# A new order of all steps in a fused attention and MLP kernel

## The chip, the cores and the metric

The kernel runs on one core of a Trainium2 chip. Its time is the device time of one execution in microseconds; three executions of the kernel before took 575.28, 575.72 and 575.73 us, median 575.72. The profiled execution has a span of 574.3 us from the first recorded instruction to the last; no other time of that execution is given, so the 1.4 us between span and median are what lies around the span.

## The reference

The input is q, k, v (batch 4, 8 heads, 768 positions, 64 dimensions) and two weights. Each query attends to the keys within 15 positions of it, and to 24 summaries, one for each block of 32 positions: the elementwise maximum of the block's keys, and the mean of its values. The attention's output, 3072 tokens by 512, goes through a GELU MLP with 2048 hidden columns.

```python
k_sum = k.reshape(B, H, nb, block, D).max(axis=3)
v_sum = v.reshape(B, H, nb, block, D).mean(axis=3)
scores_l = scale * np.matmul(q, k.transpose(0, 1, 3, 2))
mask_l = np.abs(pos[:, None] - pos[None, :]) < window
scores_s = scale * np.einsum('bhsd,bhnd->bhsn', q, k_sum) + np.log(block)
scores_all = np.concatenate([np.where(mask_l, scores_l, -1e9), scores_s], axis=-1)
a = np.exp(scores_all - scores_all.max(axis=-1, keepdims=True))
a = a / (a.sum(axis=-1, keepdims=True) + 1e-09)
x = np.matmul(a, np.concatenate([v, v_sum], axis=2))   # then to (B*S, H*D)
h = x @ w_in
out = (0.5 * h * (1.0 + erf(h / sqrt(2)))) @ w_out
```

## The kernel before

The order of all work is written by hand. ORDER is a string of 1675 step names; the program walks it once, and each step issues its few instructions. Every engine then runs its own instructions in that order: TensorE (PE), VectorE (DVE), ScalarE (ACT), GpSimd (POOL), and SyncE (SP), which issues the DMAs. An engine waits when an operand is not ready, or when the buffer that it writes is still in use; the work behind it on that engine then waits too. Buffers are few: one PSUM tile each for scores (pss), for values (psv), for sums (psd) and for the MLP's second product (pso), three for its first (psh), and four SBUF tiles of 4 KB a partition (f4k) that hold scores, maxima and raw weights in turn.

*Attention* is cut into 24 units u, each of one batch, four heads and 256 queries. Units 0 to 5 (batch 0) are computed in float32: f_mask and f_scores (TensorE, lines 656 and 688), evac (ACT copies the scores to SBUF, line 772), maximum (GpSimd, partition_all_reduce, line 785), then either m_shift (TensorE subtracts the maximum in PSUM, line 736) and m_exponent, or shift (VectorE, line 790) and exponent (ACT, line 793), f_sums and f_values (TensorE, lines 710 and 702). Later units split each operand into a float16 high and low part and multiply three times (scores, values, sums: lines 756, 838, 854; the low parts q_lo, k_lo, p_lo, v_lo on VectorE). The norm_ steps divide by the sums: norm_take and norm_spread transpose on VectorE, norm_cross copies on ACT, norm_rec and norm_mult (line 888) are VectorE's. norm_mult reads psv and so frees it. x_hi (ACT) and x_lo (VectorE, line 895) split the result for the MLP. load_vs copies the value means beside the values; for batch 0 it is a GpSimd copy (line 625), or an ACT copy in s_load_vs.

*The MLP* works on chunks c of 256 tokens, two units each. phase1 c i multiplies by 256 hidden columns (lines 915 to 917), gelu and g_hi run on ACT, g_lo on VectorE (line 933); phase2 c i multiplies by w_out (lines 1034 to 1036), store and put bring the result out. For the chunk pairs 2 to 5 the first product is done with seven instead of eight block products (sp, snap, comb, s_gelu, sg_hi, sg_lo), for the last pair the second product too (so, o_snap, o_sum, o_out, o_put).

*Weights* arrive as float64 and are cut to float32 bits on VectorE in three parts, wi_bits i 0 to 2 and wo_bits f 0 to 2: part 0 reads the raw words alone (line 386, one input), parts 1 and 2 read the raw words and the result so far (lines 391 and 395, two inputs). wi_hi and wo_hi (ACT), wi_lo and wo_lo (VectorE, lines 424 and 484) split them. This, the key summaries (prep_k, prep_k_end with a cast in line 527) and the attention of batch 0 lie in the first 105 us.

*fill* steps are three matmuls of ones each (line 337, 14 steps, and 16 such matmuls in the setup). Their result is not used.

Of the kernel before, what the change touches and what calls it, by code (L numbers as in the profile page):

```python
# [102 lines left out]
norm_mult 4, wo_bits 2 0, exponent 5, f_sums 5, prep_k_end 1 0, f_values 5, gelu 1 6, wo_bits 2 1, load_q 7, norm_take
5, wo_bits 2 2, k_lo 6, g_hi 1 7, g_lo 1 7, wo_hi 3, k_sums 1 0, wo_bits 5 0, wo_lo 3, phase1 0 6, g_lo 0 2, gelu 0 6,
g_hi 0 6, wo_bits 5 1, wo_hi 2, wo_lo 2, fetch_w_out 4 4, f_mask 6, wo_bits 4 0, wo_bits 4 1, norm_cross 5, norm_rec
5, phase1 1 2, gelu 0 7, wo_bits 4 2, wo_hi 4, wo_bits 5 2, wo_hi 5, prep_k_end 1 1, wo_lo 4, wo_lo 5, g_lo 1 4,
scores 6, fetch_v 1 0, phase2 0 1, phase2 0 3, norm_spread 5, load_k 7, s_k_hi 7, phase2 0 2, fetch_v 1 1, phase2 0 5,
g_hi 0 7, fetch_w_out 6 4, x_hi 4, fetch_w_out 7 5, x_lo 4, norm_mult 5, s_q_hi 7, prep_v 1 1, evac 6, maximum 6,
phase2 0 4, load_mask, x_hi 5, x_lo 5, load_v 7, f_mask 7, q_lo 7, gelu 1 2, k_sums 1 1, shift 6, exponent 6, phase1 2
3, g_lo 0 6, wo_bits 6 0, phase1 2 1, load_q 9, k_lo 7, gelu 2 3, wo_bits 7 0, wo_bits 6 1, scores 7, g_hi 1 2, g_lo 1  # L110
2, wo_bits 6 2, wo_bits 7 1, gelu 2 1, s_q_hi 9, wo_hi 6, g_lo 0 7, wo_lo 6, phase1 2 0, load_k 9, wo_bits 7 2, q_lo
9, phase1 2 4, s_k_hi 9, k_lo 9, fetch_v 1 3, gelu 2 0, g_hi 2 0, s_p_hi 6, wo_hi 7, wo_lo 7, phase1 2 6, load_q 11,
load_k 8, phase2 0 6, fetch_k 2 2, prep_v 1 0, g_hi 1 6, g_lo 2 0, s_q_hi 11, prep_v 1 3, q_lo 11, p_lo 6, phase2 0 7,
store 0 0, phase2 1 0, fetch_v 2 1, load_vs 6, load_q 8, evac 7, maximum 7, load_vs 7, s_k_hi 8, gelu 2 6, put 0 0,
g_lo 1 6, prep_v 2 1, sums 6, k_lo 8, fetch_k 2 0, gelu 2 4, g_hi 2 4, v_hi 6, scores 9, norm_take 6, phase2 1 2,
phase2 1 4, prep_k 2 2, shift 7, v_hi 7, v_lo 6, values 6, store 0 1, fetch_k 2 3, g_lo 2 4, g_hi 2 1, prep_k 2 0,
phase1 2 5, s_q_hi 8, q_lo 8, add_mask 9, v_lo 7, scores 8, exponent 7, s_p_hi 7, norm_cross 6, phase2 1 6, p_lo 7,
# [5 lines left out]
s_k_hi 10, phase2 1 5, x_lo 7, v_hi 9, maximum 11, phase1 3 0, v_lo 9, gelu 2 7, wt_add 1 0, wt_add 1 1, wt_add 1 2,
wt_hi 1, k_lo 10, sums 8, shift 11, values 8, s_p_hi 9, q_lo 10, norm_take 8, norm_cross 8, load_v 10, gelu 3 0, g_hi
3 0, wt_lo 1, fetch_k 3 1, load_q 12, load_vs 10, norm_rec 8, phase1 3 4, phase2 1 7, wt_add 5 0, p_lo 9, phase1 3 1,
norm_spread 8, norm_mult 8, put 1 0, g_lo 3 0, gelu 2 2, exponent 11, scores 10, wt_add 5 1, fetch_k 3 2, g_hi 2 2,
g_lo 2 2, prep_k 3 1, x_hi 8, store 1 1, wt_add 5 2, g_hi 2 7, g_lo 2 7, gelu 3 4, prep_k 3 2, values 9, wt_hi 5, sums
# [1216 lines left out]
```

## Time and profile before

| | us |
|---|---|
| median of three runs | 575.72 |
| lowest, highest | 575.28, 575.73 |
| span of the profiled execution | 574.3 |
| TensorE's last matmul ends (tail: ACT's copy, then the output's DMA) | 571.04 |

The share of the span in which an engine is busy says which one bounds the kernel; the waits of that engine say what holds it; the table by stretches says how near another engine comes to it in one part of the run. In a timeline each line gives the start, the duration, the engine, the line of the program, the operation, the tiles written and read, and the count of instructions that the line groups.

### The profile page before, as it was taken

How to read it: one execution, taken by the hardware profiler on the slowest of the kernel's cores; microseconds unless marked ns; L12 is line 12 of the kernel's file. 1: busy time of each engine (PE TensorE's matmuls, PEld its weight loads, DVE VectorE, ACT ScalarE, POOL GpSimd, SP SyncE). 2: the span in 40 equal slices, each digit the busy share in tenths (PEclk: the TensorE clock that was granted, in tenths of full speed). 3: DMA queues.
4: the chain of work that ended last, by engine and by line, in shares of the span. 5: the costliest groups of instructions: out<-in, count | busy, mean ns of one | idle time of the engine just before them, and what ended most of it. 6: DMA issues, size and time to landing. Idle time of an engine off the chain costs nothing.

```text
span 574.3 us, 13533 instructions
## 1 busy us (share of the span) xinstructions
PE 569.0 (99%) x5826; PEld 389.8 (68%) x5826; DVE 458.4 (80%) x617; ACT 379.8 (66%) x642; POOL 88.7 (15%) x42
## 2 busy tenths in 40 slices
...
GB/s 322 395 238 250 342 175 196 274 116 198 159 115 99 141 79 71 115 121 76 103 93 66 72 105 56 60 98 78 23 63 1 21 19 18 1 20 1 2 1 91
DMA packets 28652, 64.27 MB, mean 112 GB/s; under 512 B 2736, under 2 KB 7600, under 8 KB 28592
## 3 DMA queue, kind: packets, MB, share of 16 engines
...
q8 instruction: 45, 0.74, 0.5%
...
## 4 chain that ended last, share of the span: by engine, by line
PE 95%; DVE 4%; issue 1%; ACT 0%; POOL 0%; DVEq 0%; ACTq 0%; POOLq 0%
PE psy L986 15%; PE pso L1034 12%; PE pso L1035 12%; PE pso L1036 12%; PE psz L986 7%; PE psh L915 4%; PE psh L917 4%; PE psh L916 4%; PE psx L986 4%; PE pso_y L1199 4%; PE psv L838 3%; PE pss L756 3%; PE pss_x L1199 2%; PE pso_fill L337 2%; PE pss L688 1%; PE pso_fill_s L337 1%
## 5 line engine op out<-in xcount | busy, mean ns | idle before, releaser
L785 POOL PARTITION_ALL_REDUCE m<-s x23 | 77.4, 3370 | 303.5 <-DVE s L776 80.9
L1034 PE MATMUL pso<-w_out_h,gg 128*128 128x512 f16 x320 | 121.5, 380 | 0.0
L1035 PE MATMUL pso<-w_out_l,gg 128*128 128x512 f16 x320 | 121.3, 379 | 0.0
L1036 PE MATMUL pso<-w_out_h,gg 128*128 128x512 f16 x320 | 121.3, 379 | 0.0
L986 PEld LDWEIGHTS <-wt 128*128 128x128 f16 x768 | 74.4, 98 | 13.6 <-issue 1.1
L916 PE MATMUL psh<-xos,ww 128*128 128x256 f16 x256 | 69.8, 273 | 0.6 <-DVE xos L895 0.6
L915 PE MATMUL psh<-xos,ww 128*128 128x256 f16 x256 | 69.9, 273 | 0.0
L917 PE MATMUL psh<-xos,ww 128*128 128x256 f16 x256 | 69.8, 273 | 0.0
L986 PE MATMUL psy<-xos,wt 128*128 128x256 f16 x576 | 69.3, 273 | 0.0
L986 PEld LDWEIGHTS <-ww 128*128 128x128 f16 x576 | 55.4, 98 | 11.7 <-issue 0.4
L1036 PEld LDWEIGHTS <-gg 128*128 128x128 f16 x320 | 31.3, 98 | 37.8
L1034 PEld LDWEIGHTS <-gg 128*128 128x128 f16 x320 | 31.3, 98 | 33.2 <-issue 0.8
L1035 PEld LDWEIGHTS <-gg 128*128 128x128 f16 x320 | 31.3, 98 | 31.5
L1018 DVE SCALAR_TENSOR_TENSOR gg<-g,gg 128x512 f16<-128x512 f32 x48 | 34.7, 731 | 11.5 <-ACT gg L1014 11.4
L997 ACT ACTIVATE ww<-psy 128x512 f32<-128x512 f32 x48 | 28.1, 587 | 23.7 <-PE psy L986 23.4
L1041 ACT ACTIVATE ot<-pso 128x512 f32<-128x512 f32 x20 | 11.8, 592 | 29.3 <-PE pso L1036 29.3
L1014 ACT ACTIVATE gg<-g 128x512 f16<-128x512 f32 x48 | 29.4, 625 | 2.7 <-PE pso L1035 2.0
L1004 DVE TENSOR_TENSOR g<-psz,ww 128x512 f32<-128x512 f32 x24 | 16.4, 682 | 18.5 <-PE psz L986 15.8
L1011 ACT ACTIVATE g<-g 128x512 f32<-128x512 f32 x36 | 22.3, 623 | 10.8 <-DVE g L1004 10.7
L915 PEld LDWEIGHTS <-ww 128*128 128x128 f16 x256 | 25.0, 98 | 6.3 <-issue 2.2
L917 PEld LDWEIGHTS <-ww 128*128 128x128 f16 x256 | 25.0, 98 | 3.7 <-issue 0.7
L916 PEld LDWEIGHTS <-ww 128*128 128x128 f16 x256 | 25.0, 98 | 3.4
...
## 6 DMA issues: line engine op xcount, KB each, us to landing
...
```

The costliest lines, as they stand in the source:

```text
L785: nc.gpsimd.partition_all_reduce(out_ap=self.m32, in_ap=self.s32, channels=P, reduce_op=bass_isa.ReduceOp.max)
L915: nc.tensor.matmul(ph[:, e, :], wh, xh, start=(k == 0), stop=False)
L916: nc.tensor.matmul(ph[:, e, :], wh, xl, start=False, stop=False)
L917: nc.tensor.matmul(ph[:, e, :], wl, xh, start=False, stop=(k == NCC - 1))
L986: nc.tensor.matmul(ps[:, e, :], ws, xx, start=(first and e == 0 and k == 0 and m == 0), stop=(k == 1 and m == 2), skip_group_check=True,)
L997: nc.scalar.activation(snaps[b, q, n], split8(acc[b, q, "y"]), AF.Copy)
L1014: nc.scalar.activation(g_part(o // 2, q, 0, slice(o % 2, 4, 2)), g32t[b, q, o], AF.Copy, scale=SC_G)
L1018: nc.vector.scalar_tensor_tensor(out=g_part(o // 2, q, 1, fs), in0=g32t.pop((b, q, o)), scalar=SC_G, in1=g_part(o // 2, q, 0, fs), op0=ALU ...
L1034: nc.tensor.matmul(p, gh, w_out_h[:, f, :], start=(f == 0), stop=False)
L1035: nc.tensor.matmul(p, gh, w_out_l[:, f, :], start=False, stop=False)
L1036: nc.tensor.matmul(p, gl, w_out_h[:, f, :], start=False, stop=(f == NFC - 1))
L1199: nc.tensor.matmul(ps[:, j, :], g, ww_, start=(first and e == 0 and k == 0), stop=(e == 1 and k == 2), skip_group_check=True,)
```

## The change

Only ORDER is replaced. The new string holds the same 1675 steps, each once, in another order; no step's code changes. As a consequence every queue (TensorE, VectorE, ACT, GpSimd, SP) has the same instructions as before in another order, and buffers pass from step to step in another order. Steps of attention that use TensorE (f_mask, f_scores, m_shift, f_sums, f_values, scores, values, sums) stand next to each other more often; before units 2 to 5, evac and maximum stand elsewhere among VectorE's steps; the fill steps are spread. The cut below shows both orders from their start to f_values 5, and the lines around prep_k_end 2 0.

```diff
--- before.py
+++ after.py
@@ -75,167 +75,167 @@
 N_FILL_STEP = 3
 
 ORDER = '''
-fetch_k 0 0, prep_k 0 0, load_m16, f_mask 1, k_pack 0, k_pack 2, load_q 0, fetch_w_in 0 0, wi_bits 0 0, wi_bits 0 1,
-f_mask 0, fill 0, fetch_k 0 1, f_scores 0, fill 1, fill 2, fill 3, fill 4, fill 5, fill 6, fill 7, fill 8, evac 0,
-prep_k 0 1, k_pack 1, wi_bits 0 2, fetch_w_in 5 5, maximum 0, fetch_w_in 4 4, wi_bits 5 0, wi_bits 5 1, wi_hi 0, wi_lo
-0, m_shift 0, fill 9, fill 10, m_exponent 0, wi_bits 4 0, wi_bits 4 1, wi_bits 5 2, load_q 1, f_scores 1, evac 1,
-wi_bits 4 2, f_sums 0, fill 11, maximum 1, load_q 2, f_mask 2, fetch_w_in 2 2, f_scores 2, wi_hi 4, wi_hi 5, norm_take
-0, wi_bits 2 0, evac 2, load_ind, wi_bits 2 1, fetch_vt 0, sum_vt 0, norm_cross 0, norm_rec 0, maximum 2, fetch_vt 1,
-norm_spread 0, m_shift 1, m_exponent 1, fetch_vt 2, load_v 0, sum_vt 1, sum_vt 2, wi_bits 2 2, wi_hi 2, wi_lo 4,
-k_pack 3, m_shift 2, fill 12, fetch_w_in 3 3, wi_lo 5, wi_lo 2, wi_bits 3 0, load_v 1, mean_vt, wi_bits 3 1, f_sums 1,
-s_load_vs 0, f_values 0, norm_mult 0, m_exponent 2, f_mask 3, load_q 3, f_scores 3, s_load_vs 1, norm_take 1, wi_bits
-3 2, x_hi 0, x_lo 0, norm_cross 1, norm_rec 1, f_values 1, fill 13, evac 3, f_sums 2, norm_spread 1, norm_mult 1,
-norm_take 2, fetch_w_in 1 1, wi_hi 3, x_hi 1, x_lo 1, fetch_w_out 1 5, norm_cross 2, wi_bits 1 0, norm_rec 2, phase1 0
-4, wo_bits 1 0, wi_bits 1 1, load_q 6, maximum 3, m_shift 3, s_q_hi 6, wo_bits 1 1, wi_bits 1 2, phase1 0 2, fetch_k 2
-1, prep_k 2 1, load_v 2, m_exponent 3, load_vs 2, wi_hi 1, fetch_w_in 7 3, norm_spread 2, q_lo 6, phase1 0 5, f_values
-2, load_v 3, gelu 0 5, g_hi 0 5, wi_lo 1, load_vs 3, fetch_k 1 3, f_mask 4, wo_bits 1 2, gelu 0 2, load_k 4, g_hi 0 2,
-norm_mult 2, k_pack 4, f_sums 3, gelu 0 4, norm_take 3, load_q 4, norm_cross 3, prep_k 1 3, wi_bits 7 0, phase1 0 1,
-f_values 3, wi_lo 3, wi_bits 7 1, load_v 4, wo_hi 1, fetch_k 1 2, f_scores 4, x_hi 2, fetch_k 1 1, evac 4, norm_rec 3,
-norm_spread 3, g_hi 0 4, prep_k 1 2, gelu 0 1, phase1 0 0, x_lo 2, norm_mult 3, x_hi 3, fetch_w_in 6 2, prep_k 1 1,
-f_mask 5, load_vs 4, x_lo 3, g_lo 0 4, g_lo 0 5, fetch_w_out 0 4, fetch_w_out 3 5, wi_bits 6 0, phase1 0 3, maximum 4,
-shift 4, wo_lo 1, load_k 5, wi_bits 6 1, g_hi 0 1, g_lo 0 1, gelu 0 0, g_hi 0 0, g_lo 0 0, phase1 1 4, fetch_v 1 2,
-load_q 5, gelu 0 3, fetch_k 1 0, phase1 1 5, exponent 4, g_hi 0 3, wi_bits 7 2, f_values 4, gelu 1 5, wo_bits 0 0,
-wi_bits 6 2, f_sums 4, g_hi 1 5, g_lo 1 5, wi_hi 7, k_pack 5, wo_bits 0 1, norm_take 4, wi_lo 7, phase1 1 1, load_v 5,
-gelu 1 1, g_hi 1 1, g_lo 1 1, wi_hi 6, phase1 1 0, wi_lo 6, prep_v 1 2, load_vs 5, gelu 1 4, f_scores 5, phase1 1 7,
-norm_cross 4, gelu 1 0, g_hi 1 0, evac 5, g_hi 1 4, g_lo 0 3, load_k 6, s_k_hi 6, norm_rec 4, wo_bits 0 2, maximum 5,
-norm_spread 4, prep_k 1 0, g_lo 1 0, load_v 6, wo_bits 3 0, fetch_w_out 2 4, phase1 1 6, wo_hi 0, wo_bits 3 1, phase1
...
-norm_spread 6, sums 7, norm_mult 6, x_hi 6, norm_take 7, v_lo 8, phase1 2 2, maximum 9, shift 9, load_q 10, maximum 8,
-norm_mult 9, prep_k_end 2 0, maximum 10, s_q_hi 12, k_lo 12, shift 10, exponent 10, p_lo 11, q_lo 12, x_hi 9, load_k
...
+fetch_k 0 0, load_m16, fill 11, prep_k 0 0, load_q 0, f_mask 0, fill 8, load_ind, k_pack 0, fetch_w_in 0 0, f_scores
+0, k_pack 2, evac 0, fill 0, fetch_vt 0, wi_bits 0 0, fill 5, fetch_k 0 1, load_q 1, sum_vt 0, fetch_w_in 4 4, load_q
+2, maximum 0, fill 2, fetch_w_in 5 5, prep_k 0 1, wi_bits 0 1, f_mask 1, fill 9, wi_bits 0 2, fetch_vt 1, fetch_vt 2,
+wi_bits 4 0, k_pack 1, m_shift 0, m_exponent 0, wi_bits 4 1, fetch_w_in 2 2, f_scores 1, f_sums 0, f_mask 2, wi_hi 0,
+f_scores 2, evac 1, maximum 1, evac 2, maximum 2, norm_take 0, fill 4, sum_vt 1, norm_cross 0, sum_vt 2, wi_lo 0, fill
+12, m_shift 1, wi_bits 5 0, wi_bits 4 2, load_v 0, load_q 3, wi_bits 5 1, wi_hi 4, norm_rec 0, norm_spread 0, mean_vt,
+load_v 1, s_load_vs 0, fetch_w_in 1 1, m_shift 2, m_exponent 1, wi_bits 2 0, f_values 0, wi_bits 2 1, wi_bits 2 2,
+s_load_vs 1, m_exponent 2, f_sums 1, fill 1, wi_bits 5 2, norm_mult 0, f_values 1, x_hi 0, f_mask 3, norm_take 1,
+norm_cross 1, wi_lo 4, k_pack 3, fetch_w_in 3 3, fetch_w_out 1 5, f_sums 2, x_lo 0, norm_rec 1, fill 7, norm_spread 1,
+load_v 3, norm_mult 1, load_q 6, wi_hi 2, f_scores 3, x_hi 1, wi_hi 5, fetch_k 1 3, fill 3, wi_bits 1 0, x_lo 1,
+load_mask, wi_bits 3 0, norm_take 2, evac 3, maximum 3, load_vs 3, wi_lo 2, phase1 0 4, load_v 2, wi_bits 3 1,
+norm_cross 2, fetch_w_in 6 2, wi_lo 5, wi_bits 3 2, phase1 0 2, s_q_hi 6, load_k 4, norm_rec 2, load_vs 2, m_shift 3,
+q_lo 6, wi_bits 1 1, fill 10, prep_k 1 3, phase1 0 5, m_exponent 3, wo_bits 1 0, wi_bits 1 2, load_q 4, f_values 2,
+norm_spread 2, fetch_k 1 1, wo_bits 1 1, f_mask 4, wi_hi 3, wi_lo 3, gelu 0 5, f_sums 3, norm_mult 2, k_pack 4,
+f_scores 4, fetch_w_in 7 3, norm_take 3, wi_hi 1, load_k 5, wo_bits 1 2, x_hi 2, gelu 0 2, x_lo 2, wo_hi 1, load_v 4,
+wi_lo 1, norm_cross 3, f_values 3, phase1 0 3, load_q 5, evac 4, gelu 0 3, maximum 4, fetch_w_out 3 5, wo_lo 1,
+wi_bits 7 0, prep_k 1 1, k_pack 5, norm_rec 3, fetch_w_out 0 4, phase1 0 1, load_vs 4, g_hi 0 5, gelu 0 4, wi_bits 6
+0, g_hi 0 2, fill 6, wi_bits 7 1, g_hi 0 4, norm_spread 3, norm_mult 3, phase1 0 0, x_hi 3, g_lo 0 2, f_mask 5, shift
+4, wo_bits 3 0, f_scores 5, wi_bits 6 1, exponent 4, g_hi 0 3, wo_bits 0 0, f_values 4, x_lo 3, wi_bits 6 2, g_lo 0 5,
+load_v 6, f_sums 4, phase1 1 4, gelu 0 0, phase1 1 3, fetch_k 1 0, norm_take 4, load_q 7, gelu 1 4, wo_bits 0 1, fill
+13, wo_bits 0 2, fetch_k 1 2, g_lo 0 4, load_k 6, prep_k 1 0, s_q_hi 7, wo_hi 0, wi_hi 6, gelu 0 1, prep_k 1 2, wo_lo
+0, g_lo 0 3, g_hi 0 1, wi_bits 7 2, g_lo 0 1, phase1 1 0, fetch_v 1 2, wi_lo 6, phase1 1 5, gelu 1 0, prep_k_end 1 0,
+wi_hi 7, g_hi 1 0, fetch_k 2 1, norm_cross 4, wo_bits 3 1, g_hi 0 0, gelu 1 3, s_k_hi 6, g_hi 1 4, fetch_w_out 2 4,
+prep_k 2 1, wi_lo 7, evac 5, phase1 1 1, g_lo 1 4, gelu 1 5, maximum 5, g_hi 1 5, load_v 5, load_vs 5, phase1 0 6,
+prep_k_end 1 1, wo_bits 3 2, g_lo 0 0, k_lo 6, g_lo 1 5, phase1 1 2, norm_rec 4, prep_v 1 2, norm_spread 4, k_sums 1
+1, gelu 0 6, wo_bits 2 0, gelu 1 2, phase1 0 7, shift 5, fetch_w_out 5 5, wo_bits 2 1, g_lo 1 0, g_hi 0 6, exponent 5,
+wo_bits 2 2, g_hi 1 3, k_sums 1 0, phase2 0 1, norm_mult 4, wo_bits 5 0, load_k 7, s_k_hi 7, f_sums 5, norm_take 5,
+gelu 1 1, f_mask 6, fetch_w_out 4 4, wo_bits 5 1, wo_hi 3, scores 6, k_lo 7, f_values 5, norm_cross 5, wo_bits 5 2,
...
+prep_k 2 3, x_hi 6, add_mask 8, load_q 10, store 0 1, s_q_hi 10, prep_k_end 2 0, maximum 8, norm_take 7, g_hi 2 6,
...
```

## Rows read from the trace of the kernel before

**Rows 1.** The page, part 1: busy us, share of the span, instructions.

```profile
PE 569.0 (99%) x5826; PEld 389.8 (68%) x5826; DVE 458.4 (80%) x617; ACT 379.8 (66%) x642; POOL 88.7 (15%) x42
```

**Rows 2.** Waits of TensorE: line, releaser, us, times, longest us.

```profile
PE pso_fill_s L337 <- POOL warm L349: 0.9, 1, 0.9
PE psh L916 <- DVE xos L895: 0.6, 1, 0.6
```

**Rows 3.** Busy us of each engine by stretch, granted clock, DMA share, GB/s.

```profile
12.00:40.00 28.00, 27.60 (x238) 14.07 (x238) 25.16 (x26) 17.75 (x32) 9.99 (x3) 1.00 0.89 337
40.00:70.00 30.00, 29.38 (x319) 23.63 (x317) 28.99 (x35) 20.81 (x36) 11.49 (x5) 1.00 0.82 288
70.00:105.00 35.00, 35.00 (x391) 27.02 (x390) 34.90 (x43) 24.48 (x42) 6.39 (x2) 1.00 0.61 192
```

**Rows 4.** Timeline of TensorE around a scores step: start us, us.

```profile
119.02 0.27 PE L917 MATMUL psh<-xos,ww 128*128 128x256 f16 x1
119.22 0.20 PE L756 MATMUL pss<-qh,k_hi 64*128 64x64 f16 x2
...
119.90 0.19 PE L756 MATMUL pss<-qh,k_lo 64*128 64x64 f16 x2
120.03 0.28 PE L915 MATMUL psh<-xos,ww 128*128 128x256 f16 x1
```

**Rows 5.** Timeline of TensorE, consecutive fill steps.

```profile
11.10 6.89 PE L337 MATMUL pso_fill<-ones 128*64 128x512 f16 x24
17.92 1.13 PE L736 MATMUL pss<-m,neg 1*128 1x512 f32 x4
```

**Rows 6.** Timeline of TensorE before unit 5's values step.

```profile
89.56 0.38 PE L1034 MATMUL pso<-w_out_h,gg 128*128 128x512 f16 x1
89.78 0.38 PE L1035 MATMUL pso<-w_out_l,gg 128*128 128x512 f16 x1
...
92.81 1.15 PE L702 MATMUL psv<-s,v 128*64 128x64 f32 x32
```

**Rows 7.** Timeline of GpSimd: three maxima and a copy.

```profile
12.34 3.22 POOL L785 PARTITION_ALL_REDUCE m<-s  x1 [10.36 <-ACT s L772]
...
40.13 3.22 POOL L785 PARTITION_ALL_REDUCE m<-s  x1 [9.34 <-ACT s L772]
...
50.09 1.03 POOL L625 COPY v<-w_out_h 24x1024 f32<-24x1024 f32 x1 [3.47 <-DMA v<-in_vw_dram]
...
157.76 3.22 POOL L785 PARTITION_ALL_REDUCE m<-s  x1 [5.70 <-DVE s L776]
```

**Rows 8.** Timeline of VectorE beside these.

```profile
12.74 2.57 DVE L395 SCALAR_TENSOR_TENSOR wt<-gg,wt 128x1024 int32<-128x1024 int32 x1
...
42.49 1.41 DVE L386 TENSOR_SCALAR wt<-gg 128x1024 int32<-128x1024 int32 x1
...
50.25 1.42 DVE L730 TENSOR_TENSOR ql<-q,qh 128x512 f16<-128x512 f32 x1
...
158.12 2.08 DVE L933 SCALAR_TENSOR_TENSOR gg<-g,gg 128x512 f16<-128x512 f32 x1
```

**Rows 9.** Timeline of VectorE around norm_mult 4.

```profile
91.18 0.68 DVE L888 TENSOR_TENSOR x32s<-psv,dent 128x512 f32<-128x512 f32 x1
91.78 0.68 DVE L386 TENSOR_SCALAR wst<-xos 128x1024 int32<-128x1024 int32 x1
92.38 0.18 DVE L527 CAST ks<-ks 128x48 f16<-128x48 f32 x1
...
92.72 1.22 DVE L391 SCALAR_TENSOR_TENSOR wst<-xos,wst 128x1024 int32<-128x1024 int32 x1
```

**Rows 10.** VectorE's groups by form: busy us, mean ns, idle before.

```profile
L724 DVE TENSOR_TENSOR k_lo<-k,k_hi 128x640 f16<-128x640 f32 x18 | 17.1, 948 | 3.2 <-ACT k_hi L664 3.2
...
L395 DVE SCALAR_TENSOR_TENSOR wst<-x32s,wst 128x1024 int32<-128x1024 int32 x4 | 4.9, 1214 | 0.0
```

**Rows 11.** Timeline of ACT, its last instruction.

```profile
571.08 0.38 ACT L1225 ACTIVATE g_os<-pso_y 128x256 f32<-128x256 f32 x1 [4.86 <-PE pso_y L1199]
```

More of the change, by code (lines that the diff above doesn't have):

```diff
@@ L103 @@
[L103 to L117, printed above, removed]
@@ L123 @@
[L123 to L127, printed above, removed]
@@ new lines @@
+4 1, gelu 0 7, wo_lo 5, wo_bits 4 2, x_lo 4, g_hi 1 2, fetch_v 1 0, wo_hi 4, g_lo 1 2, norm_rec 5, phase1 1 7, wo_lo
+4, g_lo 1 3, norm_spread 5, phase1 1 6, fetch_w_out 7 5, g_hi 0 7, phase2 0 3, phase2 0 2, norm_mult 5, gelu 1 6,
+prep_v 1 1, evac 6, x_hi 5, x_lo 5, gelu 1 7, g_hi 1 1, g_lo 0 7, maximum 6, phase2 0 4, fetch_w_out 6 4, shift 6,
+phase2 0 5, load_v 7, phase1 2 6, phase1 2 1, prep_v 1 0, fetch_v 1 3, g_hi 1 6, exponent 6, s_p_hi 6, wo_bits 6 0,
+f_mask 7, gelu 2 1, wo_bits 6 1, prep_v 1 3, wo_bits 7 0, scores 7, s_k_hi 9, g_lo 1 6, p_lo 6, wo_bits 7 1, gelu 2 6,
@@ new lines @@
+g_lo 1 1, wo_bits 6 2, phase1 2 3, load_q 9, load_vs 7, s_q_hi 9, wo_hi 6, k_lo 9, wo_bits 7 2, gelu 2 3, g_hi 2 1,
+phase1 2 4, wo_lo 6, load_vs 6, wo_hi 7, phase1 2 0, v_hi 6, q_lo 9, fetch_k 2 3, fetch_v 2 1, wo_lo 7, v_lo 6, v_hi
+7, g_hi 1 7, g_lo 2 1, prep_v 2 1, load_k 8, fetch_v 2 2, load_q 11, phase2 0 6, sums 6, evac 7, g_lo 1 7, store 0 0,
+maximum 7, values 6, s_k_hi 8, prep_v 2 2, gelu 2 4, s_q_hi 11, fetch_k 2 2, norm_take 6, put 0 0, g_hi 2 4, q_lo 11,
+scores 9, load_q 8, shift 7, phase2 0 7, phase2 1 0, exponent 7, k_lo 8, norm_cross 6, load_k 11, v_lo 7, phase1 2 7,
@@ new lines @@
+fetch_k 2 0, prep_k 2 2, s_p_hi 7, norm_rec 6, s_q_hi 8, add_mask 9, load_v 8, load_vs 8, gelu 2 7, norm_spread 6,
+q_lo 8, p_lo 7, maximum 9, phase2 1 2, scores 8, norm_mult 6, g_hi 2 3, s_k_hi 11, load_v 9, prep_k 2 0, sums 7,
+prep_k 2 3, x_hi 6, add_mask 8, load_q 10, store 0 1, s_q_hi 10, prep_k_end 2 0, maximum 8, norm_take 7, g_hi 2 6,
+load_vs 9, values 7, x_lo 6, q_lo 10, norm_cross 7, g_hi 2 7, phase2 1 4, phase1 2 5, shift 8, norm_rec 7, shift 9,
+phase1 2 2, v_hi 8, norm_spread 7, put 0 1, exponent 8, v_lo 8, norm_mult 7, s_p_hi 8, phase2 1 6, p_lo 8, fetch_v 2
@@ new lines @@
+0, g_lo 2 7, load_v 11, fetch_k 3 1, k_lo 11, exponent 9, sums 8, g_lo 2 6, store 1 0, norm_take 8, load_vs 11, g_lo 2
+4, values 8, x_hi 7, x_lo 7, gelu 2 2, s_p_hi 9, norm_cross 8, scores 11, gelu 2 5, add_mask 11, p_lo 9, norm_rec 8,
+g_hi 2 5, prep_k_end 2 1, phase2 1 1, g_lo 2 3, load_k 10, phase1 3 1, load_q 12, prep_v 2 0, v_hi 9, s_k_hi 10,
+phase1 3 4, v_lo 9, g_hi 2 2, norm_spread 8, norm_mult 8, fetch_v 2 3, phase2 1 3, g_lo 2 2, gelu 3 4, gelu 2 0,
+values 9, k_lo 10, prep_k 3 1, put 1 0, g_lo 2 5, x_hi 8, sums 9, maximum 11, load_v 10, shift 11, s_q_hi 12, k_sums 2
```

228 lines of the change are left out of this document (113 added, 115 removed).

## The prediction

> **What bounds the kernel now.** I read the busy shares first: TensorE is busy 569.0 us of the 574.3 [rows 1]. It is the bound, so a gain can only be work or pauses taken from TensorE, and a loss only a new wait of TensorE. The view of TensorE's waits then says how little it stands: 0.9 us at the start, where nothing is ready, and one 0.6 us wait for VectorE's x_lo 1 [rows 2]. The table by stretches says who is nearly as loaded: VectorE is busy 25.16 of 28, 28.99 of 30 and 34.90 of 35 us from 12 to 105 us, while TensorE is full too [rows 3]. Up to 105 us two engines are full at once, and the order only just keeps VectorE in front. The last thing read is the tail: the last matmul ends at 571.04 and ACT's o_out and the output's DMA follow [rows 11]; so 4 x 1, o_out 1 and o_put 2 1 end both orders, so the 3.3 us of tail stay.
>
> **The change, part by part.** Both orders hold the same 1675 steps, so every engine runs the same instructions, and the sums of durations are equal. What can differ: the pauses between neighbours on TensorE, how long VectorE is held by GpSimd, and who waits.
>
> *Grouping on TensorE.* When matmuls of another tile shape follow, the pipeline pauses: 128x128 to 64x128 goes from a start at 119.02 to one at 119.22 (0.20 against 0.11 within the shape), and back from 119.90 to 120.03 (0.13 against 0.03): about 0.095 us each [rows 4]. I counted changes of shape along both orders: 137 before, 120 after. 17 x 0.095 = -1.6 us. Two fill steps in a row also pause: 24 matmuls of eight fills last from 11.10 to 17.92, 6.82 us [rows 5]; a matmul of 512 columns is 0.22 us behind the one before it (89.56, 89.78) [rows 6], so 24 need 5.2, and 1.5 us are the seven joints and the change of shape, 0.22 a joint. The old order has eight such joints, the new one two (fill 11 behind the setup, fill 5 behind fill 0): 6 x 0.22 = -1.3 us. The wait of 0.6 goes too: TensorE has fill 7, f_scores 3 and fill 3 before phase1 0 4 now, where it had fill 13 alone beside f_sums 2, so x_lo 1 has longer. Unhindered, then, 574.3 - 1.6 - 1.3 - 0.6 = 570.8 us.
>
> *VectorE beside GpSimd.* VectorE is held while GpSimd works, in two ways. A two-input operation that starts early in a maximum (3.22 us) waits until 1.75 us after the maximum's start: g_lo at 158.12 takes 2.08 instead of 0.68 beside the maximum of 157.76 and ends at 160.20; wi_bits' third part at 12.74 takes 2.57 instead of 1.21 beside the one of 12.34 [rows 7, 8, 10]. The first part of wi_bits and wo_bits (L386, one input, int32) waits longer, to 0.13 before the maximum's end: at 42.49 it takes 1.41 instead of 0.68, the maximum ending at 43.35. GpSimd's copies in load_vs hold too, to 0.13 before their end: q_lo at 50.25 takes 1.42 instead of 0.68 beside the copy of 50.09 [rows 7 to 9]. Summed so over the old rows, VectorE loses 8.0 us up to norm_mult 4 (91.18); the first three of rows 8 make 2.8 of it.
>
> [...]
>
> I walked the new order through its five queues with the duration of each operation's rows, each step released by its operands and its free buffer, and VectorE held as above. Walked so, the old order comes out at 570.7 for the last matmul (571.04 in the trace) with the one wait in its place. In the new order nine operations of VectorE fall beside GpSimd's work before norm_mult 4. Two-input beside maxima: wi_bits 0 1 0.3 (maximum 0), wi_bits 4 2 1.2 (2), wi_bits 3 1 1.7 (3), wo_bits 3 2 1.7 (5): 4.9 us. One-input beside maxima: wi_bits 5 0 3.1, since maximum 2 now follows maximum 1 at once and it stands behind both on VectorE, and wi_bits 6 0 1.9 (4): 5.0. Beside copies: wi_bits 3 2 and q_lo 6 (load_vs 3, 2), wi_bits 7 1 (4) and g_lo 1 5 (5): 2.2. Together 12.2, so 4.2 more than before.
>
> *What that does at f_values 5.* It needs the one psv buffer, which norm_mult 4 frees. TensorE reached it at 92.81 [rows 6]. In the new order the wait (0.6) and the joints (1.3) are gone ahead of it, eight more changes of shape (0.8) and f_mask 6 and scores 6 (1.15; 24 matmuls of scores run from 119.22 to 120.03 [rows 4]) come in: 92.8 again. On VectorE norm_mult 4 was instruction 87 of its queue and ended at 91.86 [rows 9], only 0.95 before it was wanted. It is now instruction 95: g_lo 0 2 and 1 4 stand for g_lo 1 1 and 1 3, and k_lo 6 (0.95), prep_k_end 1 0 and 1 1 (0.18 and about as much again, each) and wo_bits 2 0, 2 1, 2 2 (0.68, 1.22, 1.21) come in: 4.8 us [rows 9, 10], less 0.08 of overlap each (91.18 + 0.68 against 91.78), 4.2. With the same idle time on VectorE it ends at 91.86 + 4.2 + 4.2 = 100.3, and TensorE, there at 92.8, is 7.5 us late. TensorE does not take it in one piece. The walk puts it at f_values 0 (0.9) and f_values 1 (1.8, norm_mult 0), f_values 3 (2.2, norm_mult 2), f_values 4 (2.1, shift 4 and so exponent 4), and 1.8 in smaller ones up to f_values 5: 8.7 us. I take 8 between the two; bounds are 0 (nothing held: norm_mult 4 at 91.86 + 4.2 - 8.0 = 88.1) and 13 (with the whole hold).
>
> *Later.* Past 105 us VectorE has room. The walk leaves sums 8 (1.0: prep_k_end 2 0, a cast, now stands right ahead of maximum 8 and is caught by it, then p_lo 8 is late) and two scores steps (0.4): 1.4 us, between 0 and 3.
>
> *Moved for nothing.* SP's queue is permuted with the rest, its fetches of weights, k, v and q among them; the DMA share up to 70 us is 0.82 to 0.89 [rows 3]. In the old trace VectorE hardly waits for a DMA, and the walk, with the fetches in the new order, leaves none that TensorE feels: 0, at worst 2 us for one late weight. GELU, g_hi and stores on ACT are covered by its idle third [rows 1].
>
> The sum: 570.8 + 8 + 1.4 = 580.2 us against the profiled 574.3. The median of the runs is 1.4 us above that span (575.72), so 581.6 us.
>
> **Rivals.** (a) *The maxima are really clear.* If ACT and TensorE reach the maxima at other times than walked, half of the 8.0 of holds is left at most, norm_mult 4 ends by 92.1, and only the savings on TensorE count: 570.8 + 1.4 = 572.2 us, faster. For it: a shift of one maximum by 1 to 2 us frees any of the two-input ones. Against it: maxima 1 and 2 back to back hold wi_bits 5 0 wherever in their 6.4 us it starts. (b) *Only the two-input operations come clear.* Then 7.2 us of holds remain (one-input and copies), 0.8 less than before; norm_mult 4 ends at 91.86 + 4.2 - 0.8 = 95.3, a wait of 2.5, and with 1 later: 570.8 + 3.5 + 1.4 = 575.7, no change. It decides from where the holds fall under 8. [...]
>
> **How the numbers follow.** The forecast 0.72, (a) 0.17, (b) 0.08, (c) 0.03. A measurement of this kernel tells 0.2%, 1.15 us, from no change. All of the forecast's own range, 577 to 586 (waits of 4.8 to 13.8 instead of 9.4), is slower; (c) too; (a) is faster, (b) within 0.2% or little beside it. So slower 0.74, faster 0.18, same 0.08. The range 572.5 to 586 holds half of (a), (b) and all but a tenth of the forecast, some 8 in 10.
>
> **What would show it.** Right: TensorE's waits list L702 behind VectorE's L888 and ACT's exponent in the first 105 us, together 6 us or more, and TensorE is busy about 3 us less than 569.0 with them taken out; L386 has two rows of 2.5 us and more beside maxima, one of them near 3.7 beside maxima 1 and 2. The grouping is wrong if TensorE's busy time is not lower. The forecast fails if L386 starts outside the maxima, or if norm_mult 4 ends ahead of 94 us: then VectorE's idle time in front, which I took as unchanged, was smaller.

## The result and the profile after

The kernel in the new order took 583.38 us (median of 4 runs, 582.40 to 584.38) against 575.73 us, a ratio of 1.0128 with the 95% interval 1.0109 to 1.0148: slower by 7.65 us, where 5.9 was forecast, and inside the range. The four runs are two pairs, 582.4 us at a mean granted clock of 0.997 and 584.3 to 584.4 at 0.991, and the profile is of one of the second pair (584.34). Its span is 582.6 us, 8.3 more than before.

The first view is the page's busy time, which answers to [rows 1].

```profile
PE 571.6 (98%) x5826; PEld 394.3 (68%) x5826; DVE 452.6 (78%) x617; ACT 380.6 (65%) x646; POOL 92.6 (16%) x42
```

TensorE is still the bound, but busy 571.6 and not about 566 us: 2.6 more, where the grouping should have given 2.9 back. The view of TensorE's waits (line, releaser, us, times, longest us) answers to [rows 2].

```profile
PE psn L854 <- ACT ph L801: 1.5, 1, 1.5
PE pss L736 <- POOL m L785: 1.2, 1, 1.2
PE psv L702 <- DVE x32s L888: 1.0, 1, 1.0
PE psn L854 <- DVE pl L805: 1.0, 1, 1.0
PE pso_fill_s L337 <- POOL warm L349: 0.9, 1, 0.9
PE psy L986 <- ACT ww L997: 0.9, 2, 0.7
PE pso_y L1199 <- ACT g_os L1225: 0.5, 1, 0.5
```

Two waits, 0.9 and 0.6 us, have become 7.6 us in all (with two rows of 0.4 and 0.2 that are not shown here). That at L916 is gone, as forecast. The table by stretches answers to [rows 3] (columns: window, length, busy PE, PEld, DVE, ACT, POOL, granted clock, DMA share, GB/s).

```profile
12.00:40.00 28.00, 26.84 (x217) 13.23 (x218) 23.28 (x25) 16.82 (x31) 12.34 (x3) 0.88 0.99 367
40.00:70.00 30.00, 29.03 (x312) 22.80 (x311) 29.38 (x33) 19.43 (x34) 11.99 (x5) 0.94 0.69 254
70.00:105.00 35.00, 34.39 (x383) 26.79 (x382) 34.65 (x44) 26.52 (x47) 5.59 (x2) 1.00 0.55 187
```

VectorE is 1.9 us less busy in the first stretch and as full as it was in the others, but TensorE's granted clock, 1.00 before, is 0.88 and 0.94 in the first two stretches. In shorter stretches of the same view one sees where:

```profile
28.00:30.00 2.00, 0.88 (x4) 0.05 (x2) 1.95 (x2) 1.85 (x3) 1.98 (x1) 0.94 1.03 380
30.00:36.00 6.00, 5.97 (x49) 3.15 (x50) 3.96 (x5) 3.10 (x5) 0.00 (x0) 0.50 0.82 294
36.00:38.00 2.00, 2.00 (x38) 1.31 (x39) 1.97 (x4) 1.94 (x7) 0.00 (x0) 0.86 1.03 364
56.00:58.00 2.00, 1.03 (x20) 0.95 (x20) 1.90 (x4) 0.97 (x2) 0.00 (x0) 0.76 1.05 401
58.00:60.00 2.00, 2.00 (x26) 1.57 (x23) 2.00 (x3) 1.43 (x4) 0.00 (x0) 0.50 1.01 360
60.00:62.00 2.00, 2.00 (x18) 1.72 (x17) 2.00 (x3) 1.77 (x5) 0.01 (x1) 0.89 0.81 244
```

The clock is at its lower level (0.50) from 29.7 to about 36.6 us, and again from 57.0 to about 60.5. In the second stretch a 128x256 matmul starts 0.21 us behind the one before it (59.36, 59.57), after it 0.11 (60.77, 60.88). Each fall comes while TensorE stands idle: some 0.9 us into the 1.16 us ahead of m_shift 2, and at the end of the 0.97 us ahead of f_values 3. That idle time alone does not bring it, as e10 shows below. Summed over these stretches, (1 - clock) x length, my estimate of the full-rate work that was not done, is 0.1 + 3.0 + 0.3 + 0.5 + 1.0 + 0.2 = 5.1 us. That is most of the 5.5 us (2.6 + 2.9) by which TensorE's busy time lies above the forecast.

The step that the prediction's sum hung on is norm_mult 4 on VectorE and f_values 5 behind it on TensorE [rows 6, 9]. The timeline of VectorE shows the operations that GpSimd held, and last norm_mult 4:

```profile
21.77 2.38 DVE L386 TENSOR_SCALAR wt<-x32s 128x1024 int32<-128x1024 int32 x1
...
27.25 1.47 DVE L386 TENSOR_SCALAR wt<-gg 128x1024 int32<-128x1024 int32 x1
...
43.47 2.91 DVE L424 SCALAR_TENSOR_TENSOR ww<-wt,ww 128x1024 f16<-128x1024 f32 x1
...
47.60 1.35 DVE L730 TENSOR_TENSOR ql<-q,qh 128x512 f16<-128x512 f32 x1
...
63.07 1.36 DVE L386 TENSOR_SCALAR wt<-gg 128x1024 int32<-128x1024 int32 x1
...
88.96 2.38 DVE L933 SCALAR_TENSOR_TENSOR gg<-g,gg 128x512 f16<-128x512 f32 x1
...
99.03 0.68 DVE L888 TENSOR_TENSOR x32s<-psv,dent 128x512 f32<-128x512 f32 x1
```

norm_mult 4 ends at 99.71 (before 91.86, forecast 100.3), and f_values 5 starts at 99.81 (before 92.81):

```profile
99.81 1.15 PE L702 MATMUL psv<-s,v 128*64 128x64 f32 x32 [0.45 <-issue]
```

TensorE's last group of matmuls ends at 577.82 + 1.47 = 579.29, before at 571.04:

```profile
577.82 1.47 PE L1199 MATMUL pso_y<-t,gg 128*128 128x256 f16 x12 [0.47 <-ACT g_os L1225]
```

So the 8.25 us are three sums: f_values 5 stands 7.0 us later; behind it TensorE waits 3.9 us where it waited nowhere (1.51 and 0.97 at sums 8, 0.25 and 0.69 at two sp steps, 0.47 at the last so step); and the work left behind f_values 5 is 2.65 us shorter (what is left of the sum; f_mask 6 and scores 6 are already done, and there are fewer changes of shape).

### The profile page after: what moved, and what is told of

Same layout as the page of the kernel before. It is cut to its first block, busy times and chain, and to the rows that moved or that the text cites. A ratio compares the mean times of both kernels' runs of the same rounds, so it can differ in the third digit from the quotient of the medians.

```text
span 582.6 us, 13528 instructions
## 1 busy us (share of the span) xinstructions
PE 571.6 (98%) x5826; PEld 394.3 (68%) x5826; DVE 452.6 (78%) x617; ACT 380.6 (65%) x646; POOL 92.6 (16%) x42
## 4 chain that ended last, share of the span: by engine, by line
PE 71%; DVE 2%; ACT 1%; DMA 1%; issue 0%; ACTq 0%
PE psy L986 14%; PE pso L1034 10%; PE pso L1035 10%; PE pso L1036 10%; PE psz L986 7%; PE pso_y L1199 4%; PE psx L986 4%; PE psv L838 2%; PE pss L756 2%; PE pss_x L1199 2%; PE psh L915 1%; PE psh L917 1%; PE psh L916 1%; PE psn L854 1%; PE psv_z L1199 1%; DMA q<-in_qd_dram 1%
## 5 line engine op out<-in xcount | busy, mean ns | idle before, releaser
L785 POOL PARTITION_ALL_REDUCE m<-s x23 | 81.1, 3528 | 342.1 <-DVE s L776 89.0
L916 PE MATMUL psh<-xos,ww 128*128 128x256 f16 x256 | 70.1, 274 | 0.0
L986 PEld LDWEIGHTS <-ww 128*128 128x128 f16 x576 | 56.1, 98 | 10.8
L915 PEld LDWEIGHTS <-ww 128*128 128x128 f16 x256 | 25.1, 98 | 5.9 <-issue 2.1
L790 DVE TENSOR_TENSOR s<-s,m 128x1024 f32<-128x1024 f32 x20 | 24.3, 1214 | 5.7 <-POOL m L785 5.7
L805 DVE TENSOR_TENSOR pl<-s,ph 128x1024 f16<-128x1024 f32 x18 | 21.9, 1216 | 7.8 <-ACT ph L801 7.8
L916 PEld LDWEIGHTS <-ww 128*128 128x128 f16 x256 | 25.2, 98 | 3.9 <-issue 0.3
```

The lines of the kernel that those rows point to most:

```text
L785: nc.gpsimd.partition_all_reduce(out_ap=self.m32, in_ap=self.s32, channels=P, reduce_op=bass_isa.ReduceOp.max)
L915: nc.tensor.matmul(ph[:, e, :], wh, xh, start=(k == 0), stop=False)
L916: nc.tensor.matmul(ph[:, e, :], wh, xl, start=False, stop=False)
L986: nc.tensor.matmul(ps[:, e, :], ws, xx, start=(first and e == 0 and k == 0 and m == 0), stop=(k == 1 and m == 2), skip_group_check=True,)
```

## The experiments

All kernels are the new order or the old one with the edits shown; diffs are in steps of ORDER. For each profile I kept a ledger of VectorE up to norm_mult 4: its end, the time lost in holds (each row's duration above that of its own form undelayed), and the idle time. Times in us; "clock" lists the mean granted clock of the timed runs. The ledger is of one profile each: after's at 0.991, those of e2, e3, e6 and e9 at 0.997, the others at 1.00.

| kernel | median | norm_mult 4 ends | held | idle | clock |
|---|---|---|---|---|---|
| before | 575.73 | 91.86 | 7.8 | 11.3 | 1.00 |
| after | 583.38 | 99.71 | 8.1 | 15.0 | 0.991, 0.997 |
| e2 new head, old tail | 583.06 | 97.86 | 9.0 | 12.4 | 0.997, 1.00 |
| e3 new, write-only maxima | 578.28 | 92.04 | 3.4 | 12.0 | 0.997 |
| e4 old, write-only maxima | 576.17 | 90.82 | 5.3 | 12.7 | 1.00 |
| e6 s_q_hi 10 later | 579.92 | 97.78 | 9.0 | 12.3 | 0.985 to 1.00 |
| e9 e6, copies on ACT | 578.74 | 95.34 | 6.6 | 12.2 | 0.988 to 1.00 |
| e10 e6, wo_bits 2 later | 580.00 | 95.53 | 8.9 | 13.0 | 1.00 |
| e12 all causes out | 573.71 | 90.92 | 0.7 | 13.4 | 1.00, 0.991 |

### Which part of the order loses the time

```diff
 e1: old order up to and with f_values 5
+    then all other steps in the new order
 e2: new order up to and with f_values 5
+    then all other steps in the old order
```

> The old order as far as f_values 5, then all steps that are left in the new order. Theory A (the loss arises before f_values 5, by VectorE and GpSimd holding each other and TensorE's waits behind them): no loss from the head is left, 114 changes of shape instead of 137 give 2.2 us back, and the later waits of the new order (sums 8 2.5, the others 1.4) cost up to 3.9: 573.5 to 577.5 us. Rival B (the loss comes from the grouped attention of the later units): 580 to 583.

> The new order as far as f_values 5, then all steps that are left in the old order. Theory A: the waits (2.7) and the stretches of granted clock 0.5 (5.1) before f_values 5 stay, the joints of fills (1.3) stay away: 580 to 583 us. Rival B: 574 to 577.

e2 took 583.06 us (ratio 1.0123, 1.0106 to 1.0139), just above theory A's range and far from B's. The split isn't clean: in its profile f_values 5 starts at 97.96, 5.2 us later than before, and the seam adds 2.2 us of waits of its own (1.40 and 0.13 for wo_lo's w_out_l, 0.69 for a GELU). So some 5 of the 6.8 us (576.29 is the kernel before beside it) come from the new head. e1 took 590.45 us, outside both ranges, and does not answer the question: the new tail expects weights that the old head had not prepared, and TensorE waits 3.1 us for a GELU and 4.6 us for w_out's parts between 97 and 118 us. It does show that the waits at sums 8 come with the new tail (1.50 and 0.97 us there too, none in e2). A seam between two orders is a change of its own.

### Holds between VectorE and GpSimd

```diff
-            nc.gpsimd.partition_all_reduce(
-                out_ap=self.m32, in_ap=self.s32, channels=P, reduce_op=bass_isa.ReduceOp.max
-            )
+            nc.gpsimd.tensor_copy(out=self.m32[:, :1], in_=self.s32[:, :1])
+            for _ in range(3):
+                nc.gpsimd.memset(self.m32, 0.0)
```

> The new order, where each maximum is replaced by a copy of one column and three memsets of the maximum's tile (the maximum of the scores is left out of the computation): GpSimd is meant to be as busy as long, but it only writes. Theory A (holds between the two engines make the waits): maxima keep their length, the waits at m_shift 2 and f_values 3 go and the clock stays at 1.00: 572 to 576 us. Rival C (the order alone: m_shift 2 stands ahead of f_values 0 on TensorE, and VectorE has more to do before norm_mult 4): 580 to 583, with the waits in place.

> The control of the run before: the old order with the same write-only steps in place of the maxima (their values are left out). Theory A and rival C both: only the 0.6 us wait at x_lo 1 can go, 574.5 to 576 us.

The three memsets take 2.97 to 3.40 us, about a maximum's time. e3 took 578.28 us (1.0042, 1.0027 to 1.0057), e4 576.17 (0.9998, 0.9989 to 1.0007). With the copy and the memsets in place of GpSimd's maxima the new order is 5.1 us faster by the medians (4.1 against after's pair at 0.997), the old one is not: there norm_mult 4 ends 1.0 us earlier, but f_values 5 starts at 92.83 as before, and a wait of 1.0 us has come up at f_mask 5; 576.17 is 0.2 us above the range expected. norm_mult 4 now ends at 92.04, as VectorE's timeline shows:

```profile
91.35 0.69 DVE L889 TENSOR_TENSOR x32s<-psv,dent 128x512 f32<-128x512 f32 x1
```

Holds fall from 8.1 (9.0 in e6) to 3.4; waits at m_shift 2 go and that at f_values 3 falls to 0.55. Of the 3.4, 2.0 lie beside the copies and 1.5 beside memsets. The 1.5 are two one-input operations (0.68 us each when nothing holds them), so by this ledger no two-input operation lost time beside a memset:

```profile
21.04 1.38 DVE L387 TENSOR_SCALAR wt<-x32s 128x1024 int32<-128x1024 int32 x1
...
25.71 1.46 DVE L387 TENSOR_SCALAR wt<-gg 128x1024 int32<-128x1024 int32 x1
```

Theory A is right, and rival C falls for these 5 us. The miss of 2 us above the range is the 2.2 us at sums 8, still there and here followed by a half-rate stretch that costs 1.7 us of work, and the three late waits.

### The first wait, and the clock

```diff
 e5: m_shift 1, ...
-    m_shift 2, m_exponent 1, wi_bits 2 0, f_values 0, ...
+    m_exponent 1, wi_bits 2 0, f_values 0, wi_bits 2 1, wi_bits 2 2, s_load_vs 1, m_shift 2, m_exponent 2
 e7: (the new order)
+    fill 20, fill 21,
     m_shift 2
```

> The new order with one step moved: m_shift 2 stands behind f_values 0 on TensorE, no longer ahead of it (f_values 0 has all its operands when TensorE comes free at 28.9). Theory D (the 1.16 us wait for maximum 2 and the half-rate stretch that follows it set the lateness of VectorE's norm_mult 0 and all behind it): the wait goes, the clock stays at 1.00 from 28 to 40 us, norm_mult 0 comes 1.5 to 4 us earlier, and the time falls by 2 to 4.5 us to 579 to 581.5. Rival E (VectorE's own length sets f_values 5): the wait turns up at f_values 3 to 5, and the time falls by less than 1 us, 582.5 to 583.5.

> The new order with two more fill steps (1.5 us of matmuls of ones) ahead of m_shift 2, in the place where TensorE stood idle for 1.16 us; m_shift 2 can come at most 0.4 us later than before. If the granted clock falls because TensorE stood idle: no fall from 30 to 37 us, 3 us more work done there, 580.5 to 582.5 us by what VectorE lets through. If it falls for another reason: the clock falls as before, 583.4 to 584.

TensorE's first wait comes from GpSimd's side. In the profile after, the two maxima ahead of it take 4.55 and 4.66 us instead of 3.22, and at the start of each a two-input operation of VectorE was running (20.67 to 21.85, 25.21 to 26.42), which fits a wait of GpSimd for it:

```profile
20.86 4.55 POOL L785 PARTITION_ALL_REDUCE m<-s  x1 [5.39 <-ACT s L772]
25.32 4.66 POOL L785 PARTITION_ALL_REDUCE m<-wt  x1
```

m_shift 2 then starts at 30.03, when the second one is done (29.98):

```profile
30.03 1.22 PE L736 MATMUL pss<-m,neg 1*128 1x512 f32 x2 [1.16 <-POOL m L785]
```

e5 removed that wait and gained nothing: 585.37 us (582.50 to 588.48; its fastest run is level with the fastest of after, 582.40), and f_values 3 waits 1.96 us in its profile instead of 0.97. Its median is above both ranges, and its profile is of a run in which the clock fell early, so it does not decide alone; e8 (below) has the same move without that fall and speaks for rival E, by which VectorE's own length decides and TensorE's wait only moves. e7 took 587.56 (583.29 to 589.05) and doesn't answer its question, for in both profiles the clock fell earlier, at 20.3 and 20.6 us, where TensorE had stood idle for 0.1 us in all since 0.94. e10 (below) answers part of it. TensorE stands idle there for 1.15 us ahead of m_shift 2 as in after, later for 1.95 and 1.10 us ahead of f_values 3 and 4, and the clock stays up (the view is that by stretches):

```profile
28.00:30.00 2.00, 0.85 (x6) 0.06 (x2) 1.93 (x3) 1.83 (x4) 1.89 (x1) 1.00 1.04 388
30.00:36.00 6.00, 6.00 (x92) 3.37 (x92) 5.86 (x8) 4.99 (x11) 0.00 (x0) 1.00 0.87 298
```

So the clock falls in some executions and not in others after the same wait.

This is TensorE's timeline in e5, the units' float32 products in a row:

```profile
18.04 2.00 PE L688 MATMUL pss<-q,kf 64*128 64x64 f32 x32
19.97 0.84 PE L710 MATMUL psn<-s,ones_f 128*32 128x256 f32 x8
20.75 1.03 PE L656 MATMUL pss<-mask_sb 128*128 128x512 f16 x2
21.71 3.68 PE L688 MATMUL pss<-q,kf 64*128 64x64 f32 x32
```

The second f_scores step takes 3.68 us, the one before it 2.00. The same in e11 (below), by stretches:

```profile
19.00:20.00 1.00, 1.00 (x22) 0.93 (x22) 0.00 (x0) 1.00 (x3) 0.00 (x0) 1.00 1.08 422
20.00:30.00 10.00, 10.00 (x49) 5.17 (x43) 8.69 (x9) 4.09 (x10) 6.66 (x2) 0.50 1.03 393
30.00:31.00 1.00, 1.00 (x3) 0.33 (x2) 0.97 (x2) 0.00 (x0) 0.71 (x1) 0.87 1.04 387
```

Some 10.3 us at the lower level are 5.1 us of work, by the same estimate. It happens in some executions of the new order, and in none of the 17 of the kernel before that ran beside e12 (mean clock 0.999 or 1.00 in all). Where the old order has 24 fill matmuls without a pause until 17.9 us [rows 5], the new one has float32 scores, sums and scattered fills. That this brings the fall about is possible, but no run here separates it.

### ACT behind a DMA

```diff
-add_mask 8, load_q 10, store 0 1, s_q_hi 10, prep_k_end 2 0, maximum 8, ..., x_lo 6, q_lo 10, norm_cross 7
+add_mask 8, load_q 10, store 0 1, prep_k_end 2 0, maximum 8, ..., s_p_hi 9, s_q_hi 10, ..., p_lo 9, q_lo 10
```

> The new order with s_q_hi 10 and q_lo 10 moved behind unit 9's s_p_hi and p_lo. Theory F (ACT stands 6.0 us behind the DMA of load_q 10 in s_q_hi 10, and so exponent 8 and s_p_hi 8 are late): the 2.5 us of waits at sums 8 go, 580.5 to 581.5 us. Rival G (the prediction's: prep_k_end 2 0 caught by maximum 8 makes p_lo 8 late): they stay, 583 to 583.8.

> The new order with both moves, m_shift 2 behind f_values 0 and s_q_hi 10, q_lo 10 behind unit 9. If both causes are right and add up: 576 to 579 us. If another wait takes their place: 580 to 583.

The timeline of ACT after shows why sums 8 was late: ACT stood idle for 5.98 us, released by the DMA of q for unit 10, with exponent 8 and s_p_hi 8 behind it.

```profile
155.57 0.63 ACT L721 ACTIVATE qh<-q 128x512 f16<-128x512 f32 x1 [5.98 <-DMA q<-in_qd_dram]
```

e6 took 579.92 us (1.0089, 1.0058 to 1.0121), 3.5 less than after by the medians and 0.6 below the range of theory F; at the same mean clock, 0.997, it is 579.5 to 579.6 against 582.4, 2.8 less, for 2.5 us of waits. Both waits at L854 are gone from TensorE's list:

```profile
PE psv L702 <- issue: 1.6, 2, 1.1
PE pss L736 <- POOL m L785: 1.2, 1, 1.2
...
PE psy L986 <- ACT ww L997: 0.9, 2, 0.7
PE psn L710 <- ACT s L793: 0.8, 1, 0.8
PE psv L702 <- DVE x32s L888: 0.6, 1, 0.6
PE psh L915 <- ACT g L924: 0.5, 1, 0.5
```

Theory F holds, and rival G, the prediction's own cause, falls: prep_k_end 2 0 (its second instruction, 0.21 us when nothing holds it) is still caught by maximum 8 in e6, as it was in after, and no wait follows.

```profile
149.50 1.91 DVE L528 TENSOR_TENSOR ks<-ks,ks 128x48 f16<-128x48 f32 x1
```

e8, which adds e5's move, took 580.58 us, and 579.64 and 579.72 in its runs at 0.997, level with e6's: nothing on top. In its profile, without an early fall of the clock, the wait at m_shift 2 is gone and 2.23 us stand at f_values 3.

### Taking work away ahead of norm_mult 4

```diff
 e9 (on e6):
-load_vs 2, load_vs 3, load_vs 4, load_vs 5            # GpSimd
+s_load_vs 2, s_load_vs 3, s_load_vs 4, s_load_vs 5    # ACT
 e10 (on e6):
-wo_bits 2 0, ..., wo_bits 2 1, ..., wo_bits 2 2, ..., norm_mult 4
+norm_mult 4, wo_bits 2 0, wo_bits 2 1, wo_bits 2 2
 e11: both, and
-f_values 3, phase1 0 3      ...  phase2 8 4, ..., snap 5 1 1, ..., sp 5 0 1
+phase1 0 3, f_values 3      ...  snap 5 1 1, ..., phase2 8 4, sp 5 0 1
```

> The kernel of e6, with the value means of units 2 to 5 copied by ACT (s_load_vs) and no longer by GpSimd. Theory A (what VectorE loses beside GpSimd sets norm_mult 4, and norm_mult 4 the time): VectorE's holds before norm_mult 4 fall from 9.0 to about 6.5 us, norm_mult 4 ends near 95.5 instead of 97.8, and the time falls by 1.5 to 2.5 from 579.6 to 577 to 578.2. Rival H (four copies of 1.05 us more make ACT late, and TensorE waits for exponents and GELU): 579.5 to 581.

> The kernel of e6, with wo_bits 2 0, 2 1 and 2 2 (3.1 us of VectorE) moved from before norm_mult 4 to right behind it. By the prediction's step (eight instructions more ahead of norm_mult 4 cost 4.2 us) norm_mult 4 ends 2.5 to 3 us earlier, at 95; the three waits of TensorE that lie behind these instructions (0.5, 0.8, 0.4) go, 577.5 to 578.3. Rival: what is left is set before them (f_values 3 and 4): 579 to 580.

> All together, and two small moves: f_values 3 behind phase1 0 3, and phase2 8 4 between snap 5 1 1 and sp 5 0 1 (a wait of 0.7). If VectorE's lateness was the whole loss, TensorE's savings show: 573.5 to 576, level with the kernel before or a little faster. If the clock still falls or f_values 4 still waits for exponent 4: 576 to 578.5.

e9: 578.74 us (1.0071, 1.0044 to 1.0099). The ledger moved as theory A said: holds 9.0 to 6.6, norm_mult 4 from 97.78 to 95.34. The time moved 1.2 us by the medians, to 0.5 above the range of theory A, and 1.9 by the fastest runs (579.54 to 577.63); the intervals of e6 and e9 overlap, so the ledger carries the verdict here, not the time.

e10: norm_mult 4 ends 2.25 earlier, at 95.53 (2.9 with the 0.7 us more of idle time in that profile), as the eight-instruction step has it. The time is the same, 580.00 (1.0074, 1.0058 to 1.0089), and the rival is right: the wait now lies at f_values 3, behind norm_mult 2.

```profile
PE psv L702 <- DVE x32s L888: 2.0, 1, 2.0
PE pss L736 <- POOL m L785: 1.2, 1, 1.2
PE psv L702 <- issue: 1.1, 1, 1.1
```

In this profile the clock never fell, TensorE came to f_values 3 earlier, and it waited 1.95 us there instead of 0.64. norm_mult 4 was the last place where VectorE's lateness showed, not the only one.

e11 took 579.06 us (1.0079, 1.0045 to 1.0113), above both of its ranges: the two moves together with e9's and e10's gave no more than e9, the wait at the sp step stayed at 0.68, and two of five runs (582.85, whose profile has the early fall of the clock, and 583.10) have a mean clock of 0.987, the others (578.74 to 579.06) 0.997.

### The account closed

> The new order with the causes found so far taken out at once: write-only steps in place of the maxima (their values are left out), the copies of units 2 to 5 on ACT, s_q_hi 10 and q_lo 10 behind unit 9. If the account is complete, VectorE's holds before norm_mult 4 are under 1.5 us, norm_mult 4 ends by 91, TensorE's waits in the first 200 us are under 1 us, and the grouping's own savings show: 574.3 - 1.6 - 1.3 - 0.6 + 1.4 (the three late waits) + 1.7 around the span = 573.9, between 573 and 575, faster than the old order with the same write-only steps (576.2). If something else of the new order costs time: 576 or more.

```diff
 (the new order)
+write-only steps in place of the maxima (e3), s_load_vs 2 to 5 (e9), s_q_hi 10 and q_lo 10 later (e6)
```

The median is 573.71 us. Twelve runs fall into two groups: seven from 572.92 to 573.74 with a mean clock of 1.00, and five from 578.57 to 578.95 with 0.991; the ratio over both is 0.9992 (0.9963 to 1.0020). So as a whole it is level with the kernel before. Where the clock stays up (median 573.41) it is 2.9 us faster than the kernel before beside it (576.33) and 2.8 faster than e4. The page of a run of the first group, TensorE's waits, and norm_mult 4:

```profile
PE 565.9 (99%) x5826; PEld 391.5 (68%) x5826; DVE 437.9 (77%) x617; ACT 384.8 (67%) x650; POOL 81.3 (14%) x110
```

```profile
PE pso_fill_s L338 <- POOL warm L350: 0.9, 1, 0.9
PE psy L987 <- ACT ww L998: 0.9, 2, 0.7
PE pso_y L1200 <- ACT g_os L1226: 0.5, 1, 0.5
```

```profile
90.24 0.68 DVE L889 TENSOR_TENSOR x32s<-psv,dent 128x512 f32<-128x512 f32 x1
```

TensorE is busy 3.1 us less than in [rows 1]; 2.9 was forecast for changes of shape and joints. Behind the opening no wait is left before 330 us. Five of the twelve runs are 5.5 us slower all the same, about what I estimate for a mean clock of 0.991 (0.009 x 577 = 5.2); where in them the clock fell no kept profile shows. A control of the old order with the copies on ACT was not run; e4 has 1.5 us of waits left that it could lose.

## Why the prediction was right

**The grouping's gain (2.9 us)**: right in kind, its size open to 1 us. e12's busy time is 565.9 against 569.0. But e4, the old order too, is at 568.2, since its 16 opening fills take 5.71 us and not 6.56, so 2.3 is left against e4; e10, with the maxima in and the clock up, has 567.2. The joints were priced too high: to the next start a lone fill step of e12 lasts 0.76 us (15.67 to 16.43), one of eight in a row 0.85 [rows 5], so a joint avoided gives 0.09 and not 0.22, and the six some 0.5 and not 1.3.

**VectorE sets f_values 5**: right in the end time (99.71 against 100.3) and nearly in its first term, wrong in the other two. The eight further instructions, forecast at 4.2 us, cost 3.9 (99.71 - 91.86 less the change of holds and idle time); e10 takes three of them away and gets 2.9 of their 3.1 back. "With the same idle time" failed: idle time rose by 3.7 in the profile after, where norm_mult 0 waited 1.7 us for f_values 0, and that for a late maximum 2 and a slow TensorE, and by 1.0 in e6, where norm_mult 0 did not wait.

The sum of holds failed too, at "together 12.2, so 4.2 more": it was 8.1 after and 9.0 in e6, only 0.3 to 1.2 more than before. For wi_bits 5 0 the walk had 3.1 us behind two maxima; it lost 1.7 (2.38 at 21.77), and the first maximum, which started beside wi_lo 0, lasted to 25.41; that it had itself waited and was not yet under way fits this, and the prediction did not count it. wi_bits 6 0 lost 0.7 and not 1.9, wi_bits 0 1 and 4 2 nothing instead of 1.5 together. Where the walk had wi_bits 3 1 and wo_bits 3 2 caught, wi_lo 5 and g_lo 0 0, their neighbours in the queue, were caught at the same price, 1.7 each: which instruction a maximum caught could not be told from the order, the price in these two could. In sum 4.2 + 4.2 + 0 stood for 3.9 + 0.3 + 3.7. The two errors hid each other in this profile, so that its end time fits is luck. In e6's, the same program up to there, where the clock was down for a shorter time, norm_mult 4 comes at 97.78, 2.5 earlier than forecast.

**One and two inputs**: the two-input operations are not clear of the maxima. Of the five operations that a maximum caught ahead of norm_mult 4, two have two inputs (43.47, 88.96; 1.7 us each) and three have one (21.77, 27.25, 63.07; 3.2 us together); copies took 1.5 (47.60 and the next).

**TensorE's waits before f_values 5 (8)**: the total was right in the profile after, not what it is made of. There 2.7 us are idle time and 5.1 are work lost at the lower clock, 7.8; unhindered, in e12, f_values 5 starts at 91.88. The clock is a term that the prediction did not have. Its sign of being right, L702 behind L888 and the exponent with 6 us or more, did not come (1.4 in after, 3.1 in e10 at a clock of 1.00), nor did two L386 rows of 2.5 us (2.38 and 1.47 are the longest).

In e6, where f_values 5 starts at 97.88, 4.6 us stand idle: at f_values 3, 4 and 5, before f_sums 5 and in phase1 ahead of it, and 1.2 at m_shift 2, which the walk did not have; it had 2.7 at f_values 0 and 1, where nothing stands.

**What the clock costs**: a half-rate stretch of 3.4 us after 28 us cost nothing in e2: its run at 0.997 took 582.64 us and its three at 1.00 took 583.0 to 583.2. That TensorE would have waited for VectorE in that time fits this. The 10.2 us of after's profile (6.8 and 3.4) do cost: the pair at 0.991 is 2.0 us slower than the one at 0.997, and norm_mult 4 comes 1.9 later than in e6's profile. The early fall, from 20 us, costs more: 582.85 in e11's profiled run against 578.74 to 579.06.

**Later waits (1.4)**: the size was low, the cause wrong. The catch of prep_k_end 2 0 came as forecast (1.92 us at 151.42) and cost TensorE nothing; sums 8 cost 2.5 us through s_q_hi 10, which the change moved ahead of exponent 8 on ACT while its DMA was still under way (e6); I had put "moved for nothing" on SP's queue and looked for the first 70 us alone. Three waits at snap and o_out, 1.4 us, were not foreseen; the 0.4 at two scores steps did not come. These 3.9 us in place of 1.4 are more than the whole miss of 1.8 us (583.38 against 581.6).

**Rivals**: (a) needed half of the holds gone, and none went; e12 shows its number: 572.2 and the three late waits (1.4) are 573.6, within the first group. (b) falls with the holds as measured: g_lo 0 0, with two inputs, starts at 88.96 beside maximum 5 (87.91) and takes 2.38 us instead of 0.68. The 0.03 for (c) and the bound of 13 us stand for a two-input operation held to the maximum's end, and no run shows such a hold: g_lo 0 0 ends at 91.34 while the maximum lasts to 92.12, and 7.8 us, not 13, were lost ahead of f_values 5.
